# Gated linear attention with a convolutional MoE: q, k and f by feature, a VectorE scan for the decay, a compact state

## The chip, the cores and the metric

One Trainium2 chip, one core of it. The core has TensorE (PE; its weight loads are listed as PEld), VectorE (DVE), ScalarE (ACT), GpSimd (POOL) and SyncE (SP), which issues the transfers here. The metric is the device time of one execution in microseconds, the median of the runs; the profile shows one execution, instruction by instruction.

## What is computed

The inputs are q, k, v and f_logit of shape (4, 8, 768, 48): four batches, eight heads, 768 steps, 48 features. Cut to what matters:

```python
f = 1 / (1 + exp(-f_logit))
for t in range(S):                                   # per batch and head
    state = f[t][:, None] * state + outer(k[t], v[t])
    y[t] = q[t] @ state
x = y, the heads side by side                        # (4, 768, 384)
h = relu(x @ w_in)                                   # 384 -> 1024
gate = sigmoid(conv1d(h, conv_w))                    # three taps over the steps
out = (h * gate) @ w_out                             # 1024 -> 384
```

The weights come as 64-bit floats and are split on the chip into a rounded high part and a low part; a product of the second stage is three matmuls (high·high, high·low, low·high).

## The kernel before

**Chunks.** The steps are cut into chunks of 128, so there are 24 chunks (four batches of six), numbered 0 to 23. With L the running sum over a chunk of log(1 + exp(-f_logit)), k is multiplied by exp(L) and q by exp(-L); then a chunk is three products: scores (k against q, masked to the lower triangle), values (v against the masked scores), and q against the state that the chunks before have left. The state gets the chunk's k against v, and is multiplied by the decay of the chunk's last step.

**Per chunk, before.** `load_kq`, `load_f`, `load_v` bring 128 steps on the partitions, all heads beside one another; k and q are padded from 48 to 64 features a head. `gate` computes log(1 + exp(-f)) on ACT (L183, L184), for one chunk at a time in groups 0 to 2 and for three chunks at once from group 3 on, where it is also split into a rounded part and a rest (L188 on ACT, L189 on DVE). `stage_a` sums it down the partitions with a triangular matmul (L209; two of them where it is split), takes both exponentials out of PSUM (L213, L214) and multiplies k and q (L226, L227). The last row of exp(-L), which the state needs on the feature's partitions, is turned by small matmuls (L218, L222) in chunks 0 to 4 and goes through DRAM in later ones (`decay_out`, `decay_in`). `stage_b` transposes k and q, four matmuls each (L249), and copies both out of PSUM (L251). Head 2p lies on partitions 0 to 47, head 2p+1 on 64 to 111.

`scores` (L291, masked copy L293 on DVE), `state` (L305; the update is done twice per operation, once for each half of the partitions, L312 to L316) and `values` follow. In `values` the state's part is one matmul for two heads (L328): the state tile holds two 48 by 48 blocks on a 112 by 112 diagonal with zeros beside them. The scores' part is a matmul per head (L331). The result leaves PSUM as a rounded part (L339, ACT) and a rest (L340, DVE).

**The second stage.** Per half batch (384 steps), `mm1` makes the eight feature tiles of h (L368, nine matmuls each), the convolution and the gate (ACT L371, L373, L382; DVE L379, L380, L383); at the edge of a half batch GpSimd carries two columns over or clears them (L359, L361). `mm2` rounds the gated tile (L398 ACT, high part gh; L399 DVE, low part gl) and runs 24 output matmuls (L405) for 128 steps.

**What sets the order.** `plan` gives each piece of work a place (in chunks), the pieces are recorded in that order, and a scheduler then orders the instructions of each engine. From chunk 8 on, `visit` keeps the matmuls of a chunk's values, the next chunk's state and its scores together on PE. Every engine works through its own list in order, SP too. Weight splitting (`split_f64`) fills DVE and ACT early on.

Of the kernel before, what the change touches and what calls it, by code (L numbers as in the profile page):

```python
# [22 lines left out]
CFG = dict(ez="ddddddaaaavvvv", ng=8, hp=4000, tb=2, groups=[3, 3, 3, 3, 3, 3, 3, 3], sg=3, f1=2.6, g1=2.6, gv=9, gl=5.2, g=3.9, l=3.2, a=1.8, b=0.8, s=0.2, v=0.5, wil=(-2.3, -1.1), wis=(-0.7, 0.9), cw=1.3, wol=(1.3, 1.0), wos=2.1, wo=0.35, m1=0.5, m1s=0.9, m2=1.5, m2s=1.2, ek=(12, 24), ec='d', er='p', tp=0, tf=2, nw=2, gd=0, q0=2, lf=3, kpool=2, eg='d', eq='d', es='d', em='d', ew='p', xb=3, nf=6, fe='a', kb=4, qb=3, vb=4, lv=2.2, cb=1, sb=3, fi=1)  # L23

@with_exitstack
def gla_moe_kernel(ctx, tc, q_in, k_in, v_in, f_in, w_in, conv_w, w_out, out):
# [5 lines left out]
    q, k, v, f_logit = [t.rearrange("b s h d -> b h s d")[:, :, :, :D] for t in (q_in, k_in, v_in, f_in)]  # L32
# [13 lines left out]
    LR = P - 32  # L46
# [11 lines left out]
    tri32 = const.tile([P, P], F32, name="tri32")  # L58
# [7 lines left out]
    tri = const.tile([P, P], F32R, name="tri")  # L66
    nc.vector.tensor_copy(tri, tri32)
# [19 lines left out]
    ft_all = const.tile([P, B, NC, NP], F32, name="ft_all")  # L87
    nc.gpsimd.memset(ft_all, 1.0)
# [76 lines left out]
    last_exp = [None]  # L165
    group_of = [g for g, m in enumerate(groups) for _ in range(m)]
    ghl, gates, fbs, qkv, mid, tts, fts, ft_row, ready = {}, {}, {}, {}, {}, {}, {}, {}, {}

    def load_f(n):
        b, c = steps[n]  # L170
        g = group_of[n]
        if n == first[g]:
            fbs[g] = ld.tile([P, GC, H, D], F32, tag="fb", name=f"fb{g}")
        nc.sync.dma_start(fbs[g][:, n - first[g]], chunk(f_in, b, c))

    def gate(g, i, m):

        if g >= CFG["lf"] and i == 0:
            ghl[g] = [wk.tile([P, GC, DM], F32R, tag=f"cg{x}", name=f"cg{x}{g}", bufs=CFG["cb"]) for x in "hl"]
        cs = slice(i * DM, (i + m) * DM)  # L180
        fv = fbs[g].rearrange("p c h d -> p (c h d)")[:, cs]
        with tc.issue_after(last_exp[0].ins) if CFG["sg"] <= g < CFG["gd"] and g > 0 else ExitStack():
            nc.scalar.activation(fv, fv, AF.Exp, scale=-1.0)  # L183
        nc.scalar.activation(fv, fv, AF.Ln, bias=1.0)  # L184
        parts = [fv]
        if g >= CFG["lf"]:
            hi, lo = [t.rearrange("p c x -> p (c x)")[:, cs] for t in ghl[g]]
            nc.scalar.copy(hi, fv)  # L188
            (nc.vector if g < CFG["gv"] else nc.gpsimd).tensor_tensor(lo, fv, hi.bitcast(F32), ALU.subtract)  # L189
            parts = [hi, lo]  # L190
        for j in range(m):
            gates[first[g] + i + j] = [x[:, j * DM:(j + 1) * DM] for x in parts]

    def load_kq(n):
        b, c = steps[n]
        for t, src in ((kp_b[n % CFG["kb"]], k_in), (qp_b[n % CFG["qb"]], q_in)):
            nc.sync.dma_start(t, chunk(src, b, c))
# [6 lines left out]
    def stage_a(n):  # L204
        b, c = steps[n]
        gs = gates.pop(n)
        pl = ps.tile([P, DM + NP], F32, tag="s", name=f"pl{n}", bufs=3)
        for i, x in enumerate(gs):
            nc.tensor.matmul(pl[:, :DM], tri if len(gs) == 2 else tri32, x, start=(i == 0), stop=(i == len(gs) - 1))  # L209
        fd = wk.tile([P, H, D], F32, tag="fd", name=f"fd{n}")  # L210
        fi = wk.tile([P, H, D], F32, tag="fi", name=f"fi{n}", bufs=CFG["fi"])
        plv = pl[:, :DM].rearrange("p (h d) -> p h d", h=H)
        nc.scalar.activation(fi, plv, AF.Exp)  # L213
        last_exp[0] = nc.scalar.activation(fd, plv, AF.Exp, scale=-1.0)  # L214
        if n < CFG["nf"] and c < NC - 1:
            for p in range(NP):
                for j in range(2):
                    nc.tensor.matmul(pl[HP * j:HP * j + D, DM + p:DM + p + 1], fd[LR:, 2 * p + j, :],  # L218
                                     ident[LR:, P - 1:], start=True, stop=True)
            for j in range(2):  # L220
                r = slice(HP * j, HP * j + D)
                (nc.vector.tensor_copy if CFG["fe"] == "d" else nc.scalar.copy)(ft_all[r, b, c, :], pl[r, DM:])  # L222
        else:
            fts[n] = fd
        qp, kp = qp_b[n % CFG["qb"]], kp_b[n % CFG["kb"]]
        (nc.gpsimd if n < CFG["kpool"] else nc.vector).tensor_tensor(kp[:, :, :D], kp[:, :, :D], fi, ALU.mult)  # L226
        (nc.vector if CFG["eq"] == "d" or n < CFG["q0"] else nc.gpsimd).tensor_tensor(qp[:, :, :D], qp[:, :, :D], fd, ALU.mult)  # L227
# [7 lines left out]
    def decay_in(n):

        if n in ft_row:
            b, c = steps[n]
            src = ft_row.pop(n).rearrange("o (p j d) -> j d (o p)", j=2, d=D)
            for j in range(2):  # L240
                nc.sync.dma_start(ft_all[HP * j:HP * j + D, b, c, :], src[j])

    def stage_b(n):
        qp, kp = mid.pop(n)
        tt = []
        for nm, src in (("k", kp), ("q", qp)):
            pt = ps.tile([P, NP, P], F32, tag="s", name=f"pt{nm}{n}", bufs=3)
            for p in range(NP):
                nc.tensor.transpose(pt[:, p, :], src[:, 2 * p:2 * p + 2, :].rearrange("p h d -> p (h d)"), ident)  # L249
            st = wk.tile([P, NP, P], F32, tag=f"{nm}T", name=f"{nm}T{n}", bufs=CFG["tb"])  # L250
            i = (nc.vector.tensor_copy if nm == "k" and CFG["ek"][0] <= n < CFG["ek"][1] else nc.scalar.copy)(st, pt)  # L251
            ready.setdefault(n, []).append(i.ins)
            tt.append(st)
        tts[n] = (kp, tt[0], tt[1])
# [29 lines left out]
    def scores(n):  # L284
        kp, kT, qT = tts[n]
        pa = ps.tile([P, 2, NP, P], F32, tag="A", name=f"pa{n}")
        with visit(n - 1, 2):
            for p in range(NP):
                for j in range(2):
                    r = slice(HP * j, HP * j + D)  # L290
                    nc.tensor.matmul(pa[:, j, p, :], kT[r, p, :], qT[r, p, :], start=True, stop=True)  # L291
        am = a_b[n % 2]
        ready.setdefault(n, []).append(nc.vector.copy_predicated(am, mask, pa).ins)  # L293

    def state(n):
# [3 lines left out]
        kp, kT, qT = tts[n]  # L299
        vt = qkv[n]  # L300
        pk = ps.tile([P, NP, D], F32, tag="s", name=f"pk{n}", bufs=3)
        with visit(n - 1, 1):
            for p in range(NP):
                for j in range(2):
                    nc.tensor.matmul(pk[HP * j:HP * j + D, p, :], kp[:, 2 * p + j, :D], vt[:, 2 * p + j, :],  # L305
                                     start=True, stop=True)
        for j in range(2):
            r = slice(HP * j, HP * j + D)
            ft = ft_all[r, b, c, :].rearrange("p (n o) -> p n o", o=1).broadcast_to([D, NP, D])
            new = s_b[(n + 1) % 2][r, :, HP * j:HP * j + D]  # L310
            if c == 0:
                nc.vector.tensor_tensor(new, pk[r], ft, ALU.mult)  # L312
            else:
                tmp = wk.tile([P, NP, D], F32, tag="stmp", name=f"stmp{n}_{j}", bufs=1)
                nc.vector.tensor_tensor(tmp[r], pk[r], s_b[n % 2][r, :, HP * j:HP * j + D], ALU.add)
                (nc.vector if CFG["es"] == "d" else nc.gpsimd).tensor_tensor(new, tmp[r], ft, ALU.mult)  # L316

    def values(n):
        b, c = steps[n]
        kp, kT, qT = tts.pop(n)  # L320
        vt = qkv.pop(n)
        am = a_b[n % 2]
        py = ps.tile([P, NP, P], F32, tag="Y", name=f"py{n}")
        inter = c > 0 or n == 0
        with visit(n, 0):
            if inter:
                for p in range(NP):
                    nc.tensor.matmul(py[:HP + D, p, :], s_b[n % 2][:, p, :], qT[:, p, :], start=(p == 0), stop=False)  # L328
            for p in range(NP):
# [269 lines left out]
```

## Time and profile before

| | |
|---|---|
| time, median of 3 runs | 373.86 us (373.31 to 375.04) |
| profiled execution: span from first to last instruction | 369.2 us |
| profiled execution: its own time | not given apart from the span; the median lies 4.7 us above the span |
| busy PE, DVE, ACT, POOL | 348.5, 282.6, 238.0, 14.5 us |
| mean granted TensorE clock | 0.981 |
| moved by transfers | 36.04 MB |

In the page, "busy" is the time in which at least one instruction of an engine was under way. Matmuls overlap in the pipeline, so a matmul's duration in a row is longer than the time it adds; what it adds is read from the start of one group of rows to the start of the next.

### The profile page before, as it was taken

Reading aid. Unit: us, or ns where it says so; the run is one execution under the profiler, and the core shown is the slowest. Engines: PE = TensorE matmul, PEld = TensorE weight load, DVE = VectorE, ACT = ScalarE, POOL = GpSimd, SP = SyncE. Lnnn points to the kernel's source line nnn. Section 1 sums busy time; section 2 is a strip of 40 time slices with the busy share of each in tenths; the row PEclk is TensorE's granted clock in tenths of the full one; section 3 lists DMA queues with packets and bytes.
Section 4 is the critical chain, followed back from the end, with each engine's and each line's share of the span. In section 5 each row is a group of like instructions: output and inputs, shape, how many; then the busy total and the mean of one; then the engine's idle time right before and its main releaser. Section 6 shows DMA issues by size and latency. Waiting matters only on the chain.

```text
span 369.2 us, 7321 instructions
## 1 busy us (share of the span) xinstructions
PE 348.5 (94%) x2775; PEld 318.0 (86%) x2775; DVE 282.6 (77%) x482; ACT 238.0 (64%) x428; POOL 14.5 (4%) x45
## 2 busy tenths in 40 slices
PE   5799999999879999898999999999999999999993
PEld 1466768988779899897999999999999999999993
DVE  3699998999997976887778897699768875575620
ACT  3769868898966667667846566467374546665530
POOL 1110000000410000100000000000000000000000
PEclk9699999999989999999999999999999999999998
DMA  7999355325311461344113341242101002101011
GB/s 225 356 343 387 118 127 143 108 40 158 85 25 51 104 201 23 79 139 133 50 44 86 83 124 50 73 111 56 42 22 35 23 0 56 44 2 43 23 44 51
DMA packets 28853, 36.04 MB, mean 98 GB/s; under 512 B 10847, under 2 KB 20106, under 8 KB 28810
## 3 DMA queue, kind: packets, MB, share of 16 engines
q1 hardware_dynamic: 28810, 35.49, 32.3%
q8 instruction: 24, 0.39, 0.4%
q14 instruction: 19, 0.16, 0.1%
HBM read 28.37 MB, written 4.75 MB: 90 GB/s over the span
## 4 chain that ended last, share of the span: by engine, by line
PE 71%; ACT 10%; DMA 8%; DVE 6%; issue 2%; SPq 2%; ACTq 0%; DVEq 0%
PE po L405 27%; PE ph L368 21%; DMA fb<-in_f_logit_dram 5%; PE py L331 5%; PE pa L291 5%; PE py L328 4%; DMA qp<-in_q_dram 2%; PE ptq L249 2%; PE ptk L249 2%; PE pl L209 2%; PE pk L305 2%; ACT fb L184 2%; DVE g L379 1%; ACT L184 1%; DVE am L293 1%
## 5 line engine op out<-in xcount | busy, mean ns | idle before, releaser
L368 PE MATMUL ph<-xT,wi 128*128 128x384 f32 x576 | 113.7, 345 | 4.8 <-ACT hb L371 3.0
L368 PEld LDWEIGHTS ph<-xT,wi 128*128 128x128 f32 x576 | 100.6, 188 | 9.4 <-ACT hb L371 3.9
L405 PE MATMUL po<-wo,gh 128*128 128x384 f32 x384 | 100.5, 343 | 0.2 <-ACT gh L398 0.2
L405 PEld LDWEIGHTS po<-wo,gh 128*128 128x128 f32 x384 | 70.4, 190 | 0.6 <-ACT gh L398 0.3
L405 PE MATMUL po<-wo,gl 128*128 128x384 f32 x192 | 66.4, 346 | 0.0
L371 ACT ACTIVATE hb<-ph 128x384 f32<-128x384 f32 x64 | 31.3, 489 | 32.0 <-PE ph L368 31.8
L379 DVE SCALAR_TENSOR_TENSOR g<-hb,cw,g 128x384 f32<-128x384 f32 (+1 forms) x64 | 39.4, 616 | 14.6 <-ACT g L373 14.0
L399 DVE TENSOR_TENSOR gl<-g,gh 128x1024 fp32r<-128x1024 f32 (+4 forms) x34 | 30.6, 909 | 17.6 <-ACT gh L398 17.5
L398 ACT CAST gh<-g 128x1024 fp32r<-128x1024 f32 (+4 forms) x34 | 26.5, 803 | 25.5 <-PE po L405 23.2
L382 ACT ACTIVATE g<-g 128x768 f32<-128x768 f32 (+1 forms) x32 | 27.0, 842 | 23.6 <-DVE g L380 23.5
L380 DVE SCALAR_TENSOR_TENSOR g<-hb,cw,g 128x384 f32<-128x384 f32 (+1 forms) x64 | 39.5, 617 | 3.2 <-DVE g L379 0.5
L373 ACT ACTIVATE g<-hb,cw 128x384 f32<-128x384 f32 (+1 forms) x64 | 39.5, 618 | 2.2
L383 DVE SCALAR_TENSOR_TENSOR g<-g,hb 128x768 f32<-128x768 f32 (+1 forms) x32 | 30.6, 955 | 12.6 <-ACT g L382 12.5
L405 PEld LDWEIGHTS po<-wo,gl 128*128 128x128 f32 x192 | 36.5, 190 | 0.9 <-issue 0.2
L293 DVE COPY_PREDICATED am<-mask,pa 128x1024 f32<-128x1024 uint8 x24 | 31.5, 1311 | 0.2
L291 PE MATMUL pa<-qT,kT 48*128 48x128 f32 x384 | 28.4, 285 | 0.0
L331 PE MATMUL py<-am,v 128*48 128x128 f32 x384 | 27.2, 278 | 1.2 <-DVE am L293 1.2
L291 PEld LDWEIGHTS pa<-qT,kT 48*128 48x128 f32 x384 | 23.6, 187 | 3.9 <-issue 1.6
L331 PEld LDWEIGHTS py<-am,v 128*48 128x48 f32 x384 | 20.3, 123 | 5.8 <-issue 1.9
L328 PE MATMUL py<-qT,st 128*112 128x128 f32 x168 | 22.4, 274 | 0.2 <-DVE am L293 0.2
L328 PEld LDWEIGHTS py<-qT,st 128*112 128x112 f32 x168 | 20.8, 176 | 1.1 <-issue 0.5
L339 ACT CAST xT<-py 112x512 fp32r<-112x512 f32 (+1 forms) x27 | 15.8, 585 | 7.9 <-PE py L331 7.8
(106 smaller groups left out, 413.9 us busy)
## 6 DMA issues: line engine op xcount, KB each, us to landing
kp<-in_k_dram SPq DMA_DIRECT2D x24, 256.0 KB
qp<-in_q_dram SPq DMA_DIRECT2D x24, 256.0 KB
fb<-in_f_logit_dram SPq DMA_DIRECT2D x24, 192.0 KB
v<-in_v_dram SPq DMA_DIRECT2D x24, 192.0 KB
out_dram<-ob SPq DMA_DIRECT2D x24, 192.0 KB
wis<-in_moe_w_in_dram SPq DMA_DIRECT2D x6, 512.0 KB
wos<-in_moe_w_out_dram SPq DMA_DIRECT2D x8, 384.0 KB
xT<-xT SPq DMA_DIRECT2D x48, 48.0 KB
```

The lines of the kernel that those rows point to most:

```text
L291: nc.tensor.matmul(pa[:, j, p, :], kT[r, p, :], qT[r, p, :], start=True, stop=True)
L293: ready.setdefault(n, []).append(nc.vector.copy_predicated(am, mask, pa).ins)
L328: nc.tensor.matmul(py[:HP + D, p, :], s_b[n % 2][:, p, :], qT[:, p, :], start=(p == 0), stop=False)
L331: nc.tensor.matmul(py[HP * j:HP * j + D, p, :], vt[:, 2 * p + j, :], am[:, j, p, :], start=not inter and p == 0, stop=(p == NP - 1))
L368: nc.tensor.matmul(ph, wi[:, t, wl, f * P:(f + 1) * P], xts[b, hf][:, t, xl, :], start=(i == 0), stop=(i == 3 * KT - 1))
L371: nc.scalar.activation(hb[:, 2:HS + 2], ph, AF.Relu, scale=0.5)
L373: nc.scalar.activation(cv, hb[:, 1:n + 1], AF.Copy, scale=cw[:, 1, f:f + 1])
L379: nc.vector.scalar_tensor_tensor(cv, hb[:, 2:n + 2], cw[:, 2, f:f + 1], cv, ALU.mult, ALU.add)
L380: nc.vector.scalar_tensor_tensor(cv, hb[:, 0:n], cw[:, 0, f:f + 1], cv, ALU.mult, ALU.add)
L383: nc.vector.scalar_tensor_tensor(cv, cv, 1.0, h_b[:, fp:fp + 2, 1:n + 1], ALU.add, ALU.mult)
L399: nc.vector.tensor_tensor(lo, g[:, f:f + k], hi.bitcast(F32), ALU.subtract)
L405: nc.tensor.matmul(po, g[:, f, :], wo[:, f, wl, :], start=(i == 0), stop=(i == 3 * NF - 1))
```

## The change

k, q and f are laid out on the host by feature: a tile has the features on the partitions and the 128 steps along a row. Six heads (a tile has three columns of two) take 48 of each 64 partitions; the remaining 16 of each 64 hold heads 6 and 7 in three pieces, so nothing is padding. k and q come in one transfer. The running sum is now along a row and is done by a VectorE scan per chunk (384 elements a partition, with a tile of ones that is zero at the start of each 128). Both exponentials are taken in `gate`. The products of k and q are already in the layout that the scores need, so q is not transposed; k still is (three matmuls), since the state needs it by steps. Heads 6 and 7 are put together by six small SBUF-to-SBUF transfers per chunk, for k, q and the decay's last column at once; their k by steps by a GpSimd copy. The decay's last column is copied by GpSimd into the same tile, and again into the array of all decays. The state is compact (112 partitions by 4 times 48), updated once for all partitions, and its product is one matmul per head, 48 rows by 48 or 64 columns, that is a quarter of the array; a head's output half is turned round so that four consecutive heads lie in four different quarters. The kernel's PSUM pool "s" has two buffers instead of three; the output of `values` has two banks instead of one.

```diff
 def gate(g, i, m):
+    fv, fi = [t[g][:, i:i + m]... for t in (fbs, fis)]
     nc.scalar.activation(fv, fv, AF.Exp, scale=-1.0)
     nc.scalar.activation(fv, fv, AF.Ln, bias=1.0)
-    hi, lo = ...; nc.scalar.copy(hi, fv); nc.vector.tensor_tensor(lo, fv, hi, ALU.subtract)
+    for x in range(m):
+        nc.vector.tensor_tensor_scan(fs, runs, fs, 0.0, ALU.mult, ALU.add)
+    nc.scalar.activation(fi, fv, AF.Exp)
+    nc.scalar.activation(fv, fv, AF.Exp, scale=-1.0)
 def load_kq(n):
-    for t, src in ((kp_b[...], k_in), (qp_b[...], q_in)):
-        nc.sync.dma_start(t, chunk(src, b, c))
+    nc.sync.dma_start(xs[n][:, :NB, :2 * P], kq_in[b, c])
 def stage_a(n):
-    nc.tensor.matmul(pl[:, :DM], tri, x, ...)            # one or two
-    nc.scalar.activation(fi, plv, AF.Exp); nc.scalar.activation(fd, plv, AF.Exp, scale=-1.0)
-    ...
-    tensor_tensor(kp, kp, fi, ALU.mult); tensor_tensor(qp, qp, fd, ALU.mult)
+    nc.gpsimd.tensor_copy(x[:, :NB, 2 * P:2 * P + 1], fd[:, :, P - 1:])
+    nc.gpsimd.tensor_copy(ft_all[:, b, c, :], x[:, :NB, 2 * P])
+    for y, x0 in ((fi, 0), (fd, P)):
+        nc.vector.tensor_tensor(t, t, y, ALU.mult)
+    for j in range(2):
+        for i in range(NB):
+            nc.sync.dma_start(x[d0:d0 + GAP, NB, :2 * P + 1], x[s0:s0 + GAP, i, :2 * P + 1])
-def decay_out(n): ...
-def decay_in(n): ...
 def stage_b(n):
-    for nm, src in (("k", kp), ("q", qp)):               # four transposes and a copy each
+    for i in range(NB):
+        nc.tensor.transpose(pt[:, i, :], x[:, i, :P], ident)
+    copy(kp[:, :NB, :], pt)
+    nc.gpsimd.tensor_copy(last, tail)
 def state(n):
-    for j in range(2): ...                               # each operation on 48 partitions
+    r = slice(0, HP + D)                                 # each operation on 112 partitions
 def values(n):
-    for p in range(NP):
-        nc.tensor.matmul(py[:HP + D, p, :], s_b[n % 2][:, p, :], qT[:, p, :], ...)
+    for p, j in heads:
+        o = side(p, j); w = HP if o == 0 else D
+        nc.tensor.matmul(py[HP * o:HP * o + w, j, p // 2, :], st[r, p * D:p * D + w], x[r, p, P:2 * P], ...)
```

The scheduler's order moves too. First, VectorE shortly ahead of the first low part gl_0, which the first output tile waits for. Before (mswo is weight splitting, g the convolution, stmp and st the state):

```order
L115 TENSOR_TENSOR wo<-mswo_851 128x384
L380 SCALAR_TENSOR_TENSOR g_1059<-hb,cw,g_1059 128x385
L316 TENSOR_TENSOR st_99<-stmp_0_1151,ft_all 48x4x48
L379 SCALAR_TENSOR_TENSOR g_1059<-hb,cw,g_1059 128x385
L340 TENSOR_TENSOR xT_0_1054<-py_1182,xT_0_1054 112x4x128
L380 SCALAR_TENSOR_TENSOR g_1059<-hb,cw,g_1059 128x385
L399 TENSOR_TENSOR gl_0_1198<-g_689,gh_0_1197 128x1024
```

And now (fb_1010 is the gate tile of chunks 12 to 14, x_96 at this place chunk 11; gl_0 stands eleven rows below the last one shown):

```order
L190 SCALAR_TENSOR_TENSOR fb_1010<-runs,fb_1010 128x384 x3
L368 SCALAR_TENSOR_TENSOR g_978<-hb,cw,g_978 128x385
L112 SCALAR_TENSOR_TENSOR mswo_787<-wos_326,mswo_787 128x384
L294 TENSOR_TENSOR st_106<-stmp_1198,x_93 112x192
...
L329 TENSOR_TENSOR xT_0_975<-py_1087,xT_0_975 112x4x128
L215 TENSOR_TENSOR x_96<-x_96,fi_664 128x3x128
```

Ahead of gl_0 there are now 15 scans (chunks 0 to 14) and 24 products of k and q (chunks 0 to 11), where 16 products stood.

Second, PE ahead of the first output tile po_0. Before, chunk 8's transposes, chunk 7's values, chunk 9's running sum (pl) and chunk 8's scores (pa) and state (pk):

```order
L249 MATMUL ptk_1157<-ident,kp_88 128x128 x4
L249 MATMUL ptq_1164<-ident,qp_94 128x128 x4
L328 MATMUL py_1182<-qT_1033,st_100 112x128 x4
L331 MATMUL py_1182<-am_96,v_864 48x128 x8
L209 MATMUL pl_1171<-cgh_909,tri 128x384
L209 MATMUL pl_1171<-cgl_910,tri 128x384
L291 MATMUL pa_1266<-qT_1169,kT_1162 128x128 x8
L305 MATMUL pk_1282<-v_996,kp_88 48x48 x8
L405 MATMUL po_0_1201<-wo,gh_0_1197 128x384 x2
```

And now, where py_1217 is chunk 8's values and pa_1254 chunk 9's scores:

```order
L312 MATMUL py_1217<-x_93,st_105 48x128
L312 MATMUL py_1217<-x_93,st_105 64x128 x2
...
L318 MATMUL py_1217<-am_101,v_927 48x128
...
L284 MATMUL pk_1242<-v_1015,kp_90 64x48
...
L270 MATMUL pa_1254<-x_94 128x128 x8
L394 MATMUL po_0_1110<-wo,gh_0_1106 128x384 x2
L394 MATMUL po_0_1110<-wo,gl_0_1107 128x384
```

One more chunk of attention stands ahead of po_0 than before, and po_0 is no longer interrupted by two tiles of the first product after its first matmuls.

Third, GpSimd where the convolution's edges of the second half batch are copied (hb). Before, hb copies and clears alone stood there; now (kp is k by steps, completed for heads 6 and 7):

```order
L231 COPY kp_90<-kp_90 128x2x48
L231 COPY kp_89<-kp_89 128x2x48
L350 COPY hb<-hb 128x2x2
L211 COPY x_96<-fb_663 128x3
L212 COPY ft_all<-x_96 128x3
L231 COPY kp_90<-kp_90 128x2x48
L350 COPY hb<-hb 128x2x2 x2
L211 COPY x_93<-fb_1010 128x3
```

The copies that the attention needs now stand between and behind the copies that wait for the convolution.

More of the change, by code (lines that the diff above doesn't have):

```diff
@@ L65, in gla_moe_kernel @@
     nc.vector.tensor_scalar(negr, ident, -1.0, None, ALU.mult)
-    tri = const.tile([P, P], F32R, name="tri")
-    nc.vector.tensor_copy(tri, tri32)
+    runs = const.tile([P, NB * P], F32, name="runs")
+    nc.gpsimd.memset(runs, 1.0)
+    nc.gpsimd.memset(runs.rearrange("p (n t) -> p n t", t=P)[:, :, 0:1], 0.0)
     ones = const.tile([P, 1], F32, name="ones")
@@ L205, in stage_a @@
         b, c = steps[n]
[L206 to L213, printed above, removed]
@@ L214, in stage_a @@
-        last_exp[0] = nc.scalar.activation(fd, plv, AF.Exp, scale=-1.0)
-        if n < CFG["nf"] and c < NC - 1:
-            for p in range(NP):
[L217 to L224, printed above, removed]
@@ L235, in decay_in @@
[L235 to L241, printed above, removed]
-    def stage_b(n):
-        qp, kp = mid.pop(n)
-        tt = []
-        for nm, src in (("k", kp), ("q", qp)):
[L247 to L254, printed above, removed]
+        g = group_of[n]
@@ L290, in scores @@
                     r = slice(HP * j, HP * j + D)
-                    nc.tensor.matmul(pa[:, j, p, :], kT[r, p, :], qT[r, p, :], start=True, stop=True)
+                    nc.tensor.matmul(pa[:, j, p, :], x[r, p, :P], x[r, p, P:2 * P], start=True, stop=True)
         am = a_b[n % 2]
@@ L304, in state @@
                 for j in range(2):
-                    nc.tensor.matmul(pk[HP * j:HP * j + D, p, :], kp[:, 2 * p + j, :D], vt[:, 2 * p + j, :],
+                    w = HP if j == 0 else D
+                    nc.tensor.matmul(pk[HP * j:HP * j + w, p, :], kp[:, p, HP * j:HP * j + w], vt[:, 2 * p + j, :],
                                      start=True, stop=True)
[L307 to L316, printed above, removed]
+        r = slice(0, HP + D)
@@ L318, in values @@
+        ft = x[r, :, 2 * P:2 * P + 1].broadcast_to([HP + D, NP, D])
+        new, old = [t[r, :NP * D].rearrange("p (n d) -> p n d", d=D) for t in (s_b[(n + 1) % 2], s_b[n % 2])]
+        if c == 0:
+            nc.vector.tensor_tensor(new, pk[r], ft, ALU.mult)
+        else:
+            tmp = wk.tile([P, NP, D], F32, tag="stmp", name=f"stmp{n}", bufs=1)
+            nc.vector.tensor_tensor(tmp[r], pk[r], old, ALU.add)
+            nc.vector.tensor_tensor(new, tmp[r], ft, ALU.mult)
     def values(n):
```

187 lines of the change are left out of this document (109 added, 78 removed).

## The prediction

> **What bounds the kernel now.** I first read the busy time of the engines by stage (columns: stage, its length, then busy time and count for PE, PEld, DVE, ACT and POOL, the granted clock, the transfers' share and GB/s).
>
> ```profile
> 0.00:20.00 20.00, 13.18 (x56) 7.33 (x57) 11.05 (x23) 9.93 (x19) 2.84 (x16) 0.83 0.89 298
> 20.00:60.00 40.00, 38.61 (x400) 28.55 (x399) 39.10 (x87) 32.26 (x74) 1.03 (x1) 1.00 0.72 231
> 60.00:102.00 42.00, 40.17 (x337) 34.34 (x336) 39.24 (x75) 39.04 (x70) 5.01 (x4) 1.00 0.36 99
> 102.00:180.00 78.00, 73.32 (x615) 69.26 (x615) 60.89 (x96) 54.11 (x89) 3.33 (x9) 0.98 0.31 89
> 180.00:363.00 183.00, 183.00 (x1379) 178.50 (x1375) 132.29 (x206) 102.18 (x178) 2.34 (x16) 1.00 0.19 52
> ```
>
> There are two regimes. From 180 us to the end PE never rests, and VectorE has 50 us to spare; from 102 to 180 it is nearly so. Between 20 and 102 us VectorE is busy for 78.3 of 82 us. PE looks as full there, but its busy time counts matmuls that wait in the pipeline or overlap. Then I looked at where the first regime ends, in VectorE's timeline (start, duration, line, tiles):
>
> ```profile
> 99.52 0.60 DVE L380 SCALAR_TENSOR_TENSOR g<-hb,cw,g 128x385 f32<-128x385 f32 x1
> 100.05 0.34 DVE L316 TENSOR_TENSOR st<-stmp,ft_all 48x192 f32<-48x192 f32 x1
> 100.32 0.60 DVE L379 SCALAR_TENSOR_TENSOR g<-hb,cw,g 128x385 f32<-128x385 f32 x1
> 100.85 0.67 DVE L340 TENSOR_TENSOR xT<-py,xT 112x512 fp32r<-112x512 f32 x1
> 101.45 0.60 DVE L380 SCALAR_TENSOR_TENSOR g<-hb,cw,g 128x385 f32<-128x385 f32 x1
> 101.98 1.21 DVE L399 TENSOR_TENSOR gl<-g,gh 128x1024 fp32r<-128x1024 f32 x1
> ```
>
> This is the first gl, which the first output tile needs, and VectorE reaches it without a gap. So the span is VectorE's list down to the first gl, and after that PE's list. The change is priced in these two parts.
>
> **PE after the first output tile.** What a group adds is the distance between starts in PE's timeline:
>
> ```profile
> 201.79 0.60 PE L249 MATMUL ptk<-ident,kp 128*128 128x128 f32 x4
> 202.23 0.60 PE L249 MATMUL ptq<-ident,qp 128*128 128x128 f32 x4
> 202.58 0.60 PE L405 MATMUL po<-wo,gh 128*128 128x384 f32 x2
> ...
> 205.27 0.34 PE L209 MATMUL pl<-cgh,tri 128*128 128x384 f32 x1
> 205.44 0.34 PE L209 MATMUL pl<-cgl,tri 128*128 128x384 f32 x1
> 205.62 0.51 PE L405 MATMUL po<-wo,gh 128*128 128x384 f32 x2
> ...
> 207.02 1.04 PE L328 MATMUL py<-qT,st 128*112 128x128 f32 x8
> 207.99 1.08 PE L331 MATMUL py<-am,v 128*48 128x128 f32 x16
> 208.90 0.53 PE L305 MATMUL pk<-v,kp 128*48 128x48 f32 x16
> 209.35 1.16 PE L291 MATMUL pa<-qT,kT 48*128 48x128 f32 x16
> 210.45 0.45 PE L405 MATMUL po<-wo,gl 128*128 128x384 f32 x1
> ...
> 216.72 1.04 PE L328 MATMUL py<-qT,st 128*112 128x128 f32 x8
> ```
>
> Transposes take 0.79 (201.79 to 202.58), the running sum 0.35, the state's part 0.97, values 0.91, the state's product 0.45, scores 1.10. (A 32-bit matmul is two records.) Values has 16 records of half the array's width in 0.91, the state's part 8 of full size in 0.97: two halves run at once.
>
> Now each term after the change. Transposes: three of eight, 0.30. Running sum: nothing. Scores and values: as before. State's product: half of its weight loads grow from 48 to 64 columns, so I take 0.50; at no growth it is 0.45, which is 0.6 us over the kernel. State's part: 16 records of a quarter. If four run at once it is half of the 0.91, 0.46; if only two do, it is 0.91. I take 0.46, since halves by rows (scores, 16 records in 1.10) and by columns (values) overlap already, and four consecutive heads are put into four different quarters.
>
> The order has behind the first output tile, before: 15 chunks of transposes, 14 running sums, 14 state's parts, 16 values, 12 state's products, 15 scores: 11.9 + 4.9 + 13.6 + 14.6 + 5.4 + 16.5 = 66.9 us. After: 14 of transposes, 13, 15, 11 and 14: 4.2 + 6.0 + 13.7 + 5.5 + 15.4 = 44.8 us. That is **22.1 us less**, 4 to 5 us of it because one more chunk now stands ahead of the first output tile. The products of the second stage are the same.
>
> **VectorE up to the first gl.** Neighbours overlap a little, so again I count steps between starts:
>
> ```profile
> 65.33 0.55 DVE L226 TENSOR_TENSOR kp<-kp,fi 128x384 f32<-128x384 f32 x1
> 65.80 0.55 DVE L227 TENSOR_TENSOR qp<-qp,fd 128x384 f32<-128x384 f32 x1
> 66.27 0.35 DVE L103 TENSOR_SCALAR mswo<-mswo 128x384 int32<-128x384 int32 x1
> ...
> 67.53 1.30 DVE L293 COPY_PREDICATED am<-mask,pa 128x1024 f32<-128x1024 uint8 x1
> 68.72 0.67 DVE L340 TENSOR_TENSOR xT<-py,xT 112x512 fp32r<-112x512 f32 x1
> 69.31 0.61 DVE L380 SCALAR_TENSOR_TENSOR g<-hb,cw,g 128x384 f32<-128x384 f32 x1
> 69.84 0.55 DVE L105 SCALAR_TENSOR_TENSOR mswo<-wos,mswo 128x384 int32<-128x384 int32 x1
> ```
>
> A product of k or q takes 0.47, a masked copy 1.19, a low half 0.59, a convolution pass 0.53, a state operation 0.27 (100.05 to 100.32). No row shows a scan. Its lower end is one pass over 384 elements, 0.47, and in form the nearest row is the convolution's multiply and add in one pass, 0.53. Its upper end is two passes, 0.94, one to multiply and one to add. I take 0.94: in all those rows elements are independent, while here each must wait for the one before it.
>
> [...]
>
> Counted in the order down to the first gl: 15 scans, +14.1 us; 24 products of k and q for 16, +3.8; 9 masked copies for 8, +1.2; 29 convolution passes for 27, +1.1; 14 state operations for 22, each now on all partitions at once, -2.2; 8 low halves for 9, -0.6; the rest of the rounded gate gone,
>
> ```profile
> L189 DVE TENSOR_TENSOR cgl<-fb,cgh 128x1152 fp32r<-128x1152 f32 x5 | 6.8, 1357 | 0.7 <-ACT cgh L188 0.6
> ```
>
> -1.3 (a row of 1.36 less the overlap). Together +16.1 us. Of this the first scan and a product, 1.4 us, fall into the first 20 us, where VectorE idles for 9 of 20 while the loads land. So the first gl is **14.7 us later**.
>
> **What is priced at nothing.** ScalarE loses the q copies and the exponentials out of PSUM become batched ones; it is busy for 39.0 of 42 us just before 102, but its list down to the first output tile is no longer than before, so VectorE stays last. The six small transfers per chunk stand on SP ahead of loads of v and of later chunks, and wait for VectorE's products. A transfer of that kind today:
>
> ```profile
> 128.60 2.21 DMA ft<-fd
> ```
>
> They are issued right after the products, which are planned more than a chunk ahead of the scores (a chunk is 9.7 us here, 207.02 to 216.72), which hides 2.2 us and the issue of six. Without that cover each chunk would wait about 2 us. The GpSimd copies are hidden by the same lead; they are the first rival.
>
> **Sum.** 369.2 + 14.7 - 22.1 = 361.8 us of span. The page has no other time for that execution; the median lies 4.7 us above the span (373.9 - 369.2), which I leave as it is: **366.5 us**.
>
> **Rivals.** *GpSimd's copies take the lead away (slower).* Three copies per chunk now lie between gate, transfers, transposes and state. Today GpSimd's rare edge copies look like this:
>
> ```profile
> 97.82 5.42 POOL L361 COPY hb<-hb 128x4 f32<-128x4 f32 x1 [4.76 <-DVE g L383]
> ...
> 140.07 0.19 POOL L361 COPY hb<-hb 128x4 f32<-128x4 f32 x1 [17.02 <-DVE g L383]
> 148.40 1.12 POOL L361 COPY hb<-hb 128x4 f32<-128x4 f32 x1 [8.14 <-DVE g L383]
> ```
>
> Four elements take 0.19 us or, beside a busy VectorE, 1.1 and even 5.4, and these copies wait for the convolution, with the attention's copies now behind them in the same list. If two copies on the path of each of the nine first chunks take 1.12 instead of 0.19, that is 9 x 2 x 0.93 = 16.7 us on top: 383.2. It decides from 0.8 us per chunk of the front, where the 7.4 us of gain are gone. Against it: the list runs several chunks ahead. [...]
>
> *The scan is a single pass.* The front is then 15 x 0.47 = 7.0 us shorter: 359.5. For it stands the fused row of 0.53, against it the dependence.
>
> *Quarters do not run four at a time.* 13 x 0.45 = 5.9 us are lost: 372.4, hardly different from now. No row shows rows and columns split at once.
>
> **Chances.** The forecast 0.42, GpSimd 0.27, the single pass 0.18, no quarters 0.13. A range from 357 to 381 leaves out a little below the single pass and the upper half of the GpSimd case, under 2 in 10. A measurement of this kernel can tell about 0.5%, 1.9 us, from no change. Faster by more than that (below 372.0): the single pass and nearly all of the forecast, 0.58. Within it: nearly all of the quarters' case and a little of the forecast, 0.14. Slower: 0.28.
>
> **What would show it.** Right: a scan step near 0.9 us; the first gl near 117 us; PE without gaps behind it; the state's part at about 0.5 us per chunk; transposes at 0.3. Wrong: PE waiting for GpSimd or small transfers behind the first output tile; the first gl well before 110 or after 122; the state's part at 0.9 or more.

## The result and the profile after

The changed kernel is slower: 384.97 us median (382.86 to 386.31) beside 374.26 us of the kernel before on the same chip, a ratio of 1.028 (95% interval 1.024 to 1.033). The forecast was 366.5 us. The profiled execution has a span of 384.5 us in place of 369.2, with a granted clock of 0.936 in place of 0.981. Here and below, a median is that of the runs that were not disturbed, and e_none below, whose profile is of a disturbed run, is read by its time alone.

First the busy time by stage, as it was shown of the kernel before (stage, length, busy time and count of PE, PEld, DVE, ACT, POOL, clock, transfers' share, GB/s); the second row ends where the first gl is made.

```profile
20.00:60.00 40.00, 31.84 (x260) 21.20 (x260) 31.94 (x68) 19.80 (x41) 7.84 (x13) 0.79 0.54 173
60.00:118.00 58.00, 45.96 (x427) 37.91 (x423) 55.10 (x103) 49.30 (x86) 14.70 (x23) 0.93 0.34 102
118.00:180.00 62.00, 52.75 (x397) 49.78 (x399) 42.50 (x63) 35.26 (x50) 6.13 (x17) 0.85 0.31 91
180.00:260.00 80.00, 73.77 (x695) 69.56 (x692) 58.94 (x93) 42.69 (x66) 8.85 (x28) 0.98 0.29 86
```

From 20 to 60 us VectorE is busy for 31.9 of 40 us (39.1 before) and PE for 31.8 at a clock of 0.79 (38.6 at 1.00). From 118 to 260 us PE, which should have run without a gap, rests for 15.5 of 142 us and has a clock of 0.85 in the first 62 of them. So neither regime of the prediction holds there. Where the second begins, in VectorE's timeline:

```profile
117.88 1.22 DVE L388 TENSOR_TENSOR gl<-g,gh 128x1024 fp32r<-128x1024 f32 x1
```

The first gl is at 117.9 us. But from there to the end it takes 266.6 us, where the prediction had 245. The excess has two halves. PE rests for 21.3 us of it (10.6 us behind the first gl before). And its work takes longer: it is busy for 245.3 us, where the 256.6 us before less the 22.1 that the change takes out would be 234.5. Part of that second half is the granted clock. The 24 matmuls of an output tile, in the chain of work that ended last (start, length, what):

```profile
143.81 4.22 PE po L394 x24
...
172.12 7.20 PE po L394 x24
```

The first tile comes in a stretch without a gap, with a clock of 1.00 from 139 to 168 us. The second comes right behind a gap of 3.1 us, with a clock of 0.61 from 172 to 180 us, and the same work takes 3.0 us more. In the same way the first output tile takes 1.7 us more than 4.22, and the 18 matmuls at 134.06 below, behind a gap of 6.1 us, 1.7 us more than 18 such at 150.28 (3.16 us). These three places make 6.4 us. So a late load costs PE the gap and, in this trace, a lower clock behind it.

What PE waits for is in the same chain:

```profile
115.26 1.94 PE py L318 x15
117.20 0.30 SPq L197
...
117.55 0.62 SPq L220
...
118.21 0.58 SPq L181
...
119.31 3.22 DMA fb<-in_f_logit_dram
...
122.64 1.17 ACT fb L186
...
127.19 1.79 DVE fb L190 x2
...
132.60 1.03 ACT gh L387
133.63 0.39 ACT ob L397
134.06 4.83 PE ph L357 x18
```

This is read downward. PE finishes a chunk's values. Then SP gets on with its list: a kq load (L197), a small transfer (L220), a load of f (L181). ScalarE has stood since 118.1 us for that f (its idle time there is 4.5 us), then does its exponential, a table load (1.28 us) and the logarithm, waits for VectorE's scans, does two more exponentials, and only at 132.6 comes to the gh that stands behind them in its list, then to the first output copy at 133.6 (112.9 before). PE gets its next long run of work at 134.06. Over the whole execution ScalarE stood for 17.3 us for loads of f (total us, times, longest), where it had stood for 7.1:

```profile
ACT fb L186 <- DMA fb<-in_f_logit_dram: 17.3, 9, 4.5
```

```profile
ACT fb L183 <- DMA fb<-in_f_logit_dram: 7.1, 5, 3.0
```

The first line is the changed kernel, the second the kernel before. SP's own timeline shows what such a load stands behind:

```profile
36.76 14.41 SPq L220 DMA_DIRECT2D x<-x  x18
51.27 0.53 SPq L202 DMA_DIRECT2D v<-in_v_dram  x1
51.92 0.61 SPq L197 DMA_DIRECT2D x<-in_kq_dram  x1
...
58.74 2.50 SPq L220 DMA_DIRECT2D x<-x  x4
61.28 1.05 SPq L181 DMA_DIRECT2D fb<-in_f_logit_dram  x2
```

Eighteen small transfers, those of three chunks, keep SP for 14.4 us (single ones up to 1.6 us), and the next loads of v, kq and f come behind them. Back to back, a transfer of 16 rows costs SP 0.61 to 0.62 us of issue (58.74: four of 16 KB in 2.50; six of 48 KB took 3.68 in the kernel before, shown below). By that, 144 of them are some 88 us of an in-order list. And this is what SP itself waited for (total us, times, longest):

```profile
SPq L197 <- PE py L312: 21.1, 7, 5.0
SPq L220 <- DMA x<-in_kq_dram: 19.3, 9, 4.0
SPq L220 <- DVE x L215: 18.4, 11, 6.6
```

The second and third rows are the small transfers that wait for their chunk's products, and with them all that is queued behind. The first row is another thing: a kq load waits for PE. In the kernel before, the k and q tiles came free at the state's product and at the q transposes (SP waited 11.7 us and 4.2 us for these). Now one tile, x, holds both until its last reader, the product of q with the state in values (L312). There are four of them, so the load of chunk n, planned at n - 3.2, cannot start before values of chunk n - 4, planned at n - 3.5. In the same way the tile of a group of f now holds the gate until the products of its last chunk, where before it came free at the gate; there are two of them. I call these the rings of x and of f.

### The profile page after: what moved, and what is told of

Same layout as the page of the kernel before. It is cut to its first block, busy times and chain, and to the rows that moved or that the text cites. A ratio compares the mean times of both kernels' runs of the same rounds, so it can differ in the third digit from the quotient of the medians.

```text
span 384.5 us, 7174 instructions
## 1 busy us (share of the span) xinstructions
PE 335.3 (87%) x2679; PEld 299.5 (78%) x2679; DVE 276.8 (72%) x463; ACT 221.8 (58%) x368; POOL 47.7 (12%) x122
## 4 chain that ended last, share of the span: by engine, by line
PE 57%; DMA 19%; SPq 7%; ACT 7%; DVE 6%; issue 3%; POOL 0%; ACTq 0%; DVEq 0%
PE po L394 23%; PE ph L357 19%; DMA fb<-in_f_logit_dram 7%; DMA x<-in_kq_dram 5%; PE py L318 4%; PE pa L270 4%; SPq L220 4%; DMA x<-x 3%; PE py L312 3%; DMA v<-in_v_dram 2%; DVE fb L190 2%; DMA wos<-in_moe_w_out_dram 2%; DVE x L215 2%; PE pk L284 1%; SPq L181 1%
## 5 line engine op out<-in xcount | busy, mean ns | idle before, releaser
L357 PEld LDWEIGHTS ph<-xT,wi 128*128 128x128 f32 x576 | 102.8, 193 | 12.8 <-ACT ob L397 9.9
L394 PE MATMUL po<-wo,gh 128*128 128x384 f32 x384 | 103.0, 350 | 3.1 <-ACT hb L360 3.1
L394 PEld LDWEIGHTS po<-wo,gh 128*128 128x128 f32 x384 | 72.1, 196 | 4.0 <-ACT hb L360 3.4
L270 PE MATMUL pa<-x 48*128 48x128 f32 x384 | 35.1, 309 | 5.7 <-DMA x<-x 5.7
L372 DVE SCALAR_TENSOR_TENSOR g<-g,hb 128x768 f32<-128x768 f32 (+1 forms) x32 | 30.6, 956 | 10.7 <-ACT g L371 10.7
L270 PEld LDWEIGHTS pa<-x 48*128 48x128 f32 x384 | 28.0, 206 | 11.6 <-issue 5.5
L318 PE MATMUL py<-am,v 128*48 128x128 f32 (+1 forms) x384 | 29.1, 296 | 2.0 <-DVE am L272 2.0
L318 PEld LDWEIGHTS py<-am,v 128*48 128x48 f32 (+1 forms) x384 | 22.9, 140 | 6.9 <-issue 3.4
L312 PE MATMUL py<-x,st 48*48 48x128 f32 (+1 forms) x320 | 15.6, 296 | 14.3 <-DVE am L272 11.6
L215 DVE TENSOR_TENSOR x<-x,fi 128x384 f32<-128x384 f32 x24 | 13.3, 553 | 19.6 <-DMA x<-in_kq_dram 18.8
L190 DVE TENSOR_TENSOR_SCAN fb<-runs,fb 128x384 f32<-128x384 f32 x24 | 21.7, 944 | 5.4 <-ACT fb L187 4.7
```

The source lines that it names most:

```text
L190: nc.vector.tensor_tensor_scan(fs, runs, fs, 0.0, ALU.mult, ALU.add)
L270: nc.tensor.matmul(pa[:, j, p, :], x[r, p, :P], x[r, p, P:2 * P], start=True, stop=True)
L318: nc.tensor.matmul(py[HP * o:HP * o + w, j, p // 2, :], lhs, am[:, j, p, :], start=not inter and p < 2, stop=(p >= 2))
L357: nc.tensor.matmul(ph, wi[:, t, wl, f * P:(f + 1) * P], xts[b, hf][:, t, xl, :], start=(i == 0), stop=(i == 3 * KT - 1))
L372: nc.vector.scalar_tensor_tensor(cv, cv, 1.0, h_b[:, fp:fp + 2, 1:n + 1], ALU.add, ALU.mult)
L394: nc.tensor.matmul(po, g[:, f, :], wo[:, f, wl, :], start=(i == 0), stop=(i == 3 * NF - 1))
```

## Experiments

Each ratio is against the kernel before, run on the same chip beside it, with its 95% interval; these differ a little from the quotient of the medians, and comparisons between kernels of different runs go by the ratios.

The theory after the first reading: SP's list. Rival A: VectorE's longer front, the scans above all. Rival B: GpSimd's copies. Rival C, for the merged transfers: not the issue but the landing counts.

### What stands in SP's list

Without the small transfers (`e_none`):

```
-        for j in range(2):
-            for i in range(NB):
-                ...
-                nc.sync.dma_start(x[d0:d0 + GAP, NB, :2 * P + 1], x[s0:s0 + GAP, i, :2 * P + 1])
+        # in the setup: nc.gpsimd.memset(t[:, NB, :2 * P + 1], 0.0)
```

> The changed kernel without the six small transfers per chunk: the fourth column of x is zeroed once at the start, so heads 6 and 7 give nothing. Theory (SP's list: 144 small transfers at 0.62 us of issue each, 89 us in all, and their waits on VectorE's products stand ahead of the loads of f, kq and v): the 22 us by which the stretch behind the first gl is longer than predicted (266.6 for 244) go, and some of VectorE's idle time in the front; 355 to 367 us. Rival A (VectorE's longer front, the scans above all): within 3 us of 385. Rival B (GpSimd's copies, which all stay): within 3 us of 385.

Two in place of six (`e_merge`), from 16 rows of three columns into 48 rows; the tail copy of kp follows the new order of rows:

```
-            for i in range(NB):
-                ...
-                nc.sync.dma_start(x[d0:d0 + GAP, NB, :2 * P + 1], x[s0:s0 + GAP, i, :2 * P + 1])
+            nc.sync.dma_start(x[d0:d0 + NB * GAP, NB, :2 * P + 1], x[s0:s0 + GAP, :NB, :2 * P + 1])
```

> The changed kernel with two small transfers per chunk of 48 rows each in place of six of 16 (row 3p+i of the fourth column takes row p of column i, and GpSimd's tail copy follows that order); the same bytes, the whole result. Theory (SP's issue time per transfer): 96 issues of 0.62 us fewer, 59 of 89 us, so two thirds of what leaving them out gives: 366 to 374 us. Rival C (not the issue but the landing, 1.8 us, and the waits on the products count): 382 to 386. Rivals A and B: 382 to 386.

The loads on ScalarE (`e_actq`), and in the same way those of f and v:

```
-        nc.sync.dma_start(xs[n][:, :NB, :2 * P], kq_in[b, c])
+        nc.scalar.dma_start(xs[n][:, :NB, :2 * P], kq_in[b, c])
```

> The changed kernel with the loads of f, kq and v issued by ScalarE, so that they no longer stand behind the small transfers in SP's list; the transfers stay as they are. Theory: the late loads go, 362 to 375 us, less what ScalarE pays for 72 issues (24 x (0.33 + 0.60 + 0.33) = 30 us of its list, 8% of the span, with waits for free buffers on top). Rivals A, B and C: 385 or slower.

The small transfers on GpSimd (`e_poolq`):

```
-                nc.sync.dma_start(x[d0:d0 + GAP, NB, :2 * P + 1], x[s0:s0 + GAP, i, :2 * P + 1])
+                nc.gpsimd.dma_start(x[d0:d0 + GAP, NB, :2 * P + 1], x[s0:s0 + GAP, i, :2 * P + 1])
```

> The changed kernel with the six small transfers per chunk issued by GpSimd in place of SP. Theory (SP's list): SP is as free as without them, 360 to 376 us, if GpSimd's list, busy for 48 of 385 us, bears 144 issues. Rival B (GpSimd's list is what is late): its list grows by 144 entries, slower than 390 us. Rival A: within 3 us of 385.

The last column is the time that ScalarE stood for loads of f in the profiled execution.

| kernel | us | ratio (interval) | wait for f, us |
|---|---|---|---|
| changed kernel | 385.0 | 1.028 (1.024 to 1.033) | 17.3 |
| e_none | 382.5 | 1.027 (1.016 to 1.038) | |
| e_merge | 380.1 | 1.027 (1.015 to 1.039) | 16.8 |
| e_actq | 382.8 | 1.027 (1.018 to 1.035) | 14.9 |
| e_poolq | 377.9 | 1.015 (1.008 to 1.022) | 9.3 |

The theory by itself fell, and its expectation was missed all four times: leaving the transfers out brought nothing that can be told apart, two transfers in place of six brought no more, and neither did the loads on ScalarE's list, which has work of its own. Only the transfers' move to GpSimd brought something, 1.3%. Rivals A and C are not told apart by these four. Rival B fell with that run as what bounds the changed kernel, since GpSimd had 144 entries more in its list and the kernel became faster. Its issuing group (count, busy us, mean ns, idle before it), and then two of SP's waits, in that kernel:

```profile
L220 POOL DMA_DIRECT2D x<-x x144 | 70.1, 494 | 45.9 <-DVE x L215 32.5 <-issue 3.8 <-PE ph L357 2.0
```

```profile
SPq L197 <- PE py L312: 36.9, 8, 10.0
...
SPq L181 <- DVE x L215: 20.2, 6, 5.0
```

With SP free, its loads no longer stand behind transfers; they stand for their buffers. The kq loads now wait 36.9 us for PE's product (21.1 in the changed kernel), the loads of f 20.2 us for the products of the group two before. That gave the second theory: list and rings lie one behind the other, and to open one alone shows the other. The size of such a wait is no price, though: with six buffers of x in poolq_c6 below, SP stood even 82.1 us for the same product, in a faster kernel. It costs only where somebody needs the load that comes late.

### The rings

Six buffers of x (`c6`: `cb=4` becomes `cb=6`); the same without the small transfers (`none_c6`); five of x and three of f's group (`c5f3`, three buffers of the tile fb); six of x with GpSimd's issuing (`poolq_c6`), and later five and three with GpSimd's issuing (`poolq_c5f3`). The edit of c5f3:

```
-CFG = dict(... vb=4, lv=2.2, cb=4)
+CFG = dict(... vb=4, lv=2.2, cb=5)
-            fbs[g] = ld.tile([P, GC, NB, P], F32, tag="fb", name=f"fb{g}")
+            fbs[g] = ld.tile([P, GC, NB, P], F32, tag="fb", name=f"fb{g}", bufs=3)
```

> The changed kernel with six buffers of x in place of four; nothing else. New theory (the ring: one tile now holds k and q from the load to the last reader, the product of q with the state in values, planned at n+0.5; so the load of chunk n, planned at n-3.2, waits for PE to finish values of chunk n-4, planned at n-3.5, and PE's own delay comes back to it a load, two products and a masked copy later): the waits of kq loads for py (21 us in the changed kernel, 78 without the small transfers) go, 366 to 376 us. If SP's list alone were it: 382 to 386. If VectorE's longer front were it: 382 to 386.

> Six buffers of x and no small transfers (the fourth column of x is zeroed once, heads 6 and 7 give nothing). If the ring and SP's list both hold the loads up, one behind the other: 356 to 366 us, clearly below six buffers alone. If only the ring: as six buffers alone, within 3 us. If neither (VectorE's front): 380 to 386.

> The changed kernel with five buffers of x and three of the group of f (two before; the tile now holds the gate until the products of its last chunk, so the load of a group waits for VectorE's products of two groups earlier). If f's ring counts beside x's: 362 to 372 us, below six buffers of x. If only x's ring counts: as six buffers or a little slower, 366 to 378. VectorE's front alone: 382 to 386.

> The small transfers issued by GpSimd and six buffers of x. Ring and SP's list both: 360 to 370 us, below either alone. If GpSimd's issuing already brought all there is (377.9 us): within 3 us of that.

> GpSimd issues the small transfers, five buffers of x and three of the group of f. If f's ring of two still holds loads up: 364 to 368 us. If not: 369 to 374 us, as with six buffers of x or a little slower.

| kernel | us | ratio (interval) | wait for f, us |
|---|---|---|---|
| c6 | 381.3 | 1.019 (1.010 to 1.027) | 22.1 |
| none_c6 | 378.0 | 1.012 (1.005 to 1.020) | 13.5 |
| c5f3 | 380.4 | 1.020 (1.011 to 1.028) | 19.5 |
| poolq_c6 | 370.1 | 0.989 (0.981 to 0.996) | 5.5 |
| poolq_c5f3 | 367.5 | 0.987 (0.980 to 0.993) | 4.7 |

The rings alone bring 0.9 and 0.8%, which the intervals hardly part from nothing, GpSimd's issuing alone 1.3%, five and three buffers with GpSimd's issuing 4.1%. That is the pattern of two waits in a row. Not all of it fits: c6 and c5f3 came out slower than the ring theory had them, and none_c6, with no transfers and six buffers, took 378.0 us where 356 to 366 were expected for two waits in a row. The two kernels with GpSimd's issuing came out about as expected (370.1 for 360 to 370, 367.5 for 364 to 368). Why the rings alone do so little is in SP's timeline of c5f3:

```profile
36.73 13.81 SPq L220 DMA_DIRECT2D x<-x  x18
50.64 0.53 SPq L202 DMA_DIRECT2D v<-in_v_dram  x1
```

The front is as it was: free buffers do not help a load that stands behind eighteen transfers. With GpSimd issuing, the same stretch of poolq_c5f3:

```profile
40.64 0.55 SPq L197 DMA_DIRECT2D x<-in_kq_dram  x1
41.64 0.81 SPq L181 DMA_DIRECT2D fb<-in_f_logit_dram  x2
```

### Does VectorE's list set the front?

The scans left out, once of the changed kernel (`e_noscan`) and once of poolq_c6 (`noscan_pq6`):

```
         for x in range(m):
             fs = fbs[g][:, i + x].rearrange("p n t -> p (n t)")
-            nc.vector.tensor_tensor_scan(fs, runs, fs, 0.0, ALU.mult, ALU.add)
+            pass
```

> The changed kernel with the 24 scans left out and nothing else (the log decay is not summed, the output is not the reference's). If VectorE's list set the first output tile there, as the prediction had it: 12 us less, as without the small transfers on SP and with six buffers (370.1 to 357.7): 371 to 374 us. If late loads set it: the scans lie in waits, 379 to 385 us.

> GpSimd issues the small transfers, six buffers of x, and the 24 scans are left out (the log decay is then not summed along the chunk, the output is not the reference's). If VectorE's list bounds the way to the first output tile, as the prediction had it: 15 scans x 0.94 = 14 us less than with them (370.1), 354 to 358 us. If loads, GpSimd and the order of the lists bound it: 364 to 370 us.

Of the changed kernel: 383.9 us, 1.027 (1.020 to 1.034), no difference that can be told. Of poolq_c6: 357.7 us, 0.959 (0.955 to 0.963), 3.0% or some 11 us less. One edit, two answers: in the changed kernel VectorE stood for loads in the front anyway, and 14 us of work could be taken out of its list without an effect on the time (the first gl came at 115.0 in place of 117.9); with the loads on time the list is the bound, and the work counts (102.5 in place of 115.2). The row of 20 to 60 us, of poolq_c6:

```profile
20.00:60.00 40.00, 29.21 (x261) 19.02 (x260) 38.13 (x75) 26.05 (x55) 34.56 (x60) 0.82 0.73 232
```

VectorE is busy for 38.1 of 40 us there (31.9 in the changed kernel). So rival A is wrong for the changed kernel and fits its repaired form. One thing goes with it there: without the scans ScalarE no longer waits for them in the middle of the gate, 10.7 us in all in poolq_c6, and the two were not separated.

### The same load on the old kernel

Six transfers more per chunk on SP, in the kernel before (`before_x6`):

```
         mid[n] = (qp, kp)
+        for i in range(6):
+            r = slice(GAP * i, GAP * i + GAP)
+            nc.sync.dma_start(dmy[0][r], kp[r].rearrange("p h d -> p (h d)")[:, :2 * P + 1])
```

> The kernel before with six transfers more per chunk on SP, of the same shape (16 x 257 from the k product into a tile that nothing reads), right behind the products. If SP's list by itself makes loads late: 381 to 387 us (up to 144 x 0.62 us of issue and the waits for the products). If it does so only where the loads have no lead (there the k and q tiles come free at the state's part and the q transposes, over a chunk before the load is planned): 374 to 377 us.

377.9 us, 1.010 (1.006 to 1.015): about 4 us. The expectation's upper case, 381 and more, did not come, and the lower one is a little exceeded. The same issue time costs something even where loads have a lead of over a chunk: ScalarE stood for 16.6 us for f (7.1 without the transfers). The 1.0% cannot be told from the 1.3% that the move to GpSimd is worth in the changed kernel; it is less than the 7.4% with the long rings below.

### The order of the lists, and a kernel faster than both

Two merged transfers per chunk on GpSimd with six buffers of x (`mergepq_c6`), and both rings without any transfers (`none_c5f3`):

> Two merged transfers per chunk, issued by GpSimd, and six buffers of x. If GpSimd's list (126 us busy with 144 issues of 0.49 us) is now among what is late: 364 to 368 us. If not: 368 to 372 us.

> No small transfers (heads 6 and 7 give nothing), five buffers of x, three of the group of f. If GpSimd's issuing is free of charge: 365 to 370 us, as with GpSimd issuing (367.5). If the transfers still cost through their landing and GpSimd's list: 358 to 364 us. If the order that the scheduler makes of the other lists weighs more than either: above 371.

mergepq_c6 took 382.0 us, 1.023 (1.019 to 1.028): 12 us more than poolq_c6, which issues three times as many transfers. Both expectations fell. ScalarE's timelines of the two differ in one place. First poolq_c6, then mergepq_c6; the gate is that of chunks 18 to 20 in both:

```profile
125.63 0.47 ACT L397 COPY ob<-po 128x384 f32<-128x384 f32 x1
...
133.21 1.17 ACT L186 ACTIVATE fb<-fb 128x1152 f32<-128x1152 f32 x1 [0.24 <-DMA fb<-in_f_logit_dram]
```

```profile
126.52 1.16 ACT L186 ACTIVATE fb<-fb 128x1152 f32<-128x1152 f32 x1 [7.14 <-DMA fb<-in_f_logit_dram]
...
137.47 0.47 ACT L396 COPY ob<-po 128x384 f32<-128x384 f32 x1
```

In poolq_c6 the first output copy stands ahead of that gate, in mergepq_c6 behind it, and ScalarE stands for 7.1 us for a load of f before it. Every edit lets the scheduler order the lists anew, and where a late load is about, the order decides what is caught behind it. That this alone makes the 12 us was not tried by itself. ScalarE's whole wait for f is 19.7 us in mergepq_c6 and 5.5 in poolq_c6. This wait runs through all runs: in the kernels made from the changed one, with the scans in, a time below 378 us goes with 12.3 us of it or less, and one of 378 us and more with 13.5 or more. e_merge, e_actq and none_c6 are of the second kind, so there the loads of f stayed late although SP had less to issue. That is a pattern over one profile of each kernel, not an experiment, and it does not say why the loads stayed late there. What can be said of the transfers comes from none_c5f3: 369.5 us, 0.988 (0.981 to 0.996), with 8.2 us of wait for f, the same as poolq_c5f3 within the intervals. With both rings longer, the transfers on GpSimd cost nothing that can be told from their absence.

Then the group of f was cut to two chunks with four buffers, and x to six (`g2`), all with GpSimd's issuing; `g2b` plans the loads earlier, `g2_c4` has four of x, `g2_sp` issues on SP:

```
-groups=[3, 3, 3, 3, 3, 3, 3, 3], sg=3 ... cb=4
+groups=[2] * 12, sg=4 ... cb=6
-            fbs[g] = ld.tile([P, GC, NB, P], F32, tag="fb", name=f"fb{g}")
+            fbs[g] = ld.tile([P, GC, NB, P], F32, tag="fb", name=f"fb{g}", bufs=4)
-                nc.sync.dma_start(x[d0:d0 + GAP, NB, ...
+                nc.gpsimd.dma_start(x[d0:d0 + GAP, NB, ...
```

> GpSimd issues the small transfers, six buffers of x, f in groups of two with four buffers (the last groups' tiles come free one group later than with three groups of three). Ring theory: PE's wait at 122 to 142 us, some 12 us, shrinks: 357 to 364 us, less what 4 gates more cost ScalarE in table loads (1.28 us each). If what is left is VectorE's list: 365 to 370 us.

> As g2, with two buffers of the second gate tile and the loads planned earlier (f 6.2 chunks ahead in place of 5.2, k and q 4.0 in place of 3.2). If the place in SP's list matters beside the rings: 355 to 362 us, below g2. If only the rings do: as g2 within 3 us.

> As g2 (363.1 us), with x left at four buffers. If x's ring counts beside f's: 368 to 376 us. If f's ring was all that was left: 362 to 366 us.

> As g2 (363.1 us), with the small transfers issued by SP again. If SP's list costs by itself (18 transfers in a row keep the loads back for 14 us in the front): 372 to 380 us. If the long rings give the loads enough lead: 362 to 367 us.

| kernel | us | ratio (interval) | wait for f, us |
|---|---|---|---|
| g2 | 363.1 | 0.969 (0.963 to 0.976) | 5.7 |
| g2_c4 | 370.2 | 0.987 (0.980 to 0.994) | 12.3 |
| g2_sp | 387.0 | 1.043 (1.035 to 1.052) | 17.0 |
| g2b | 374.6 | 1.006 (1.002 to 1.011) | 11.9 |

g2 is faster than both kernels: 3.1% below the kernel before, 22 us below the changed one. With GpSimd issuing, longer rings go with 2.6% (x, poolq_c6), 2.8% (f, in groups of two, g2_c4) and 4.6% together. With SP issuing in their company everything is lost again: 7.4% between g2 and g2_sp, more than expected; why it is even slower than the changed kernel was not followed up. g2b, with nothing changed but the planned place of the loads, loses 12 us, against what was expected: an earlier place in the list is no gain in itself. Its cause was not followed up either. Since a new plan of the same work alone moves 12 us, the 2.6 and 2.8% are not the prices of these two rings by themselves; that the list and the rings count together stands on the whole row, from 1.028 to 0.969. The stages of g2:

```profile
20.00:60.00 40.00, 28.54 (x211) 17.65 (x206) 38.02 (x74) 30.28 (x59) 29.32 (x58) 0.79 0.71 231
...
110.00:180.00 70.00, 64.65 (x564) 60.20 (x563) 56.22 (x85) 46.98 (x74) 29.21 (x64) 0.98 0.30 89
180.00:260.00 80.00, 80.00 (x756) 75.78 (x756) 61.47 (x97) 42.79 (x69) 21.94 (x55) 1.00 0.24 70
```

These are the prediction's two regimes: VectorE is busy for 38.0 of 40 us in the front, and PE has no gap from 180 to 260 us and few from 110.

## Why the prediction was wrong, step by step

**The scan: right.** Its group in the changed kernel, and three in a row in VectorE's timeline:

```profile
L190 DVE TENSOR_TENSOR_SCAN fb<-runs,fb 128x384 f32<-128x384 f32 x24 | 21.7, 944 | 5.4 <-ACT fb L187 4.7
```

```profile
126.31 2.66 DVE L190 TENSOR_TENSOR_SCAN fb<-runs,fb 128x384 f32<-128x384 f32 x3 [2.66 <-ACT fb L187]
```

A step of 0.89 us (2.66 / 3) was taken as 0.94, an estimate of two passes at the 0.47 of a product. The rival of a single pass, 0.47, is out.

**PE's terms: right but for the state's.** A chunk in PE's timeline, behind the first output tile:

```profile
262.69 0.66 PE L312 MATMUL py<-x,st 48*48 48x128 f32 x16
263.29 1.09 PE L318 MATMUL py<-am,v 128*48 128x128 f32 x16
264.20 0.63 PE L284 MATMUL pk<-v,kp 128*48 128x48 f32 x16
264.76 1.16 PE L270 MATMUL pa<-x 48*128 48x128 f32 x16
265.85 2.91 PE L357 MATMUL ph<-xT,wi 128*128 128x384 f32 x15
...
268.60 0.49 PE L227 MATMUL pt<-ident,x 128*128 128x128 f32 x3
268.85 0.42 PE L394 MATMUL po<-wo,gh 128*128 128x384 f32 x1
```

By the steps between starts the state's part takes 0.60 (0.46 was said), values 0.91 (0.91), the state's product 0.56 (0.50), scores 1.09 (1.10), transposes 0.25 (0.30). With the prediction's counts that is 14 x 0.25 + 13 x 0.60 + 15 x 0.91 + 11 x 0.56 + 14 x 1.09 = 46.4 us, where it had 44.8. Quarters do run together (0.91 was the price if not); the state's part is mis-sized by 1.8 us and the state's product by 0.7, and the transposes give 0.7 back.

**The first gl at 117 us: right in number, for another reason.** It came at 117.9. But VectorE had 8 us of idle time between 20 and 60 us in place of being full, and without the scans the time was the same. Up to the first gl VectorE was busy for 100.3 of 118 us, where it had been for 89.4 of 102: 10.9 of the 16 us are work, the rest is waiting. The sum of VectorE's work happened to agree with what late loads made of it; that is luck.

**"Priced at nothing": the step that failed.** "They are issued right after the products, which are planned more than a chunk ahead of the scores, which hides 2.2 us and the issue of six. Without that cover each chunk would wait about 2 us." Three things in it are wrong. The price: a cover for the transfer was weighed, not one for what stands behind it. (The 2.2 us were read from ft<-fd, one row written to DRAM; the new transfers took 1.8 from issue to landing.) In the list of SP six transfers are 3.7 us, and three chunks' took 14.4 us, for loads that ScalarE and VectorE wait for in order. The issue time stood in the trace of the kernel before, in the six xT transfers on SP:

```profile
79.96 3.68 SPq L345 DMA_DIRECT2D xT<-xT  x6
```

The lead: it was read from the plan, and a plan says when a load may be issued, not when its buffer is free. That x lives until values, and f's tile until the products, was in the diff and in no term of the sum. The place: "each chunk would wait" took the cost for a toll per chunk, while it falls where a late load stands ahead of other work in an in-order list, as in 118 to 134 us. What the runs showed in its place: with the transfers out of SP's list and longer rings (poolq_c5f3, g2) the time is below that of the kernel before, and neither alone brings it there.

**PE's list priced at full clock: wrong.** The sum took PE's steps from stretches without a gap. Behind the gaps that the late loads make, PE had a clock of 0.61 (172 to 180 us) to 0.70 (119.9 to 125.9), and three such places cost 6.4 us beside the gaps themselves.

**ScalarE "no longer than before, so VectorE stays last": right in the length, wrong in what follows.** Up to the first output copy ScalarE was busy for 88.6 us, before for 87.5. But it stands for late loads of f, the gate now waits for VectorE's scans in the middle, and the first output copy stands behind it.

**GpSimd's copies (383.2 us): near in number, wrong in kind.** The chain of the changed kernel:

```profile
PE 57%; DMA 19%; SPq 7%; ACT 7%; DVE 6%; issue 3%; POOL 0%; ACTq 0%; DVEq 0%
```

GpSimd has no share in it, and more work for it made the kernel faster. Its copies took 0.48, 0.38 and 0.65 us in the mean (L211, L212, L231), where the rival had 1.12.

**The sum.** 361.8 us of span were forecast. poolq_c5f3, which restores the cover that the sum assumed, has 365.5, and g2 361.7. That g2 meets the sum so closely is partly luck: its first gl is at 113.8, 3 us earlier than forecast, the rest takes 247.9, 3 us longer, and its groups of f are other ones. The terms were those of a kernel whose loads come in time, and this one's do not.

## What to carry to other kernels

When an edit works in place, look for each buffer's last reader before and after it: a tile that lives longer takes the lead from the load that refills it, whatever the plan says (here SP stood for 21.1 us at the kq loads for the last reader of x, L312). Price a small transfer by what it costs its queue's list (0.61 us here) and by who waits for the loads behind it, not by its own landing (1.8 us). And where two causes lie one behind the other, neither alone shows much (here 1.3 and 0.8%, and 4.1% together): test them together before a theory is dropped. A gap in PE is to be priced with the clock behind it, where the trace shows that the clock falls (here to 0.61 from 172 to 180 us).

## What the runs showed of the hardware

A small transfer of 48 rows cost its issuing queue as much as one of 16. In e_merge, two of 48 rows:

```profile
21.52 1.22 SPq L219 DMA_DIRECT2D x<-x  x2
```

That is 0.61 us for 48 rows, as for 16. A load of v, 128 rows with 1.5 KB each, took 0.33 at the least and 0.39 in the median, and GpSimd 0.49 for the small transfer (its group above). SP's issue of a small transfer took 0.61 us beside 1.8 from issue to landing (the median of the 144), a third, and moving it to another list went with 1.3% less time with the old rings and 7.4% less with the long ones. What that issue time cost showed here not at the transfer but at the loads behind it: ScalarE stood for 17.3 us for f with the transfers on SP and for 9.3 with them on GpSimd (e_poolq).
